# Weight conversion: first Prelu pass dense in float32, second pass in place, hi parts rounded by VectorE

## The chip, the cores and the metric

The kernel runs on one core of one Trainium2 chip. The metric is the device time of one execution in microseconds (us). It is measured several times for each kernel, and the median is given. The engines are PE (TensorE: matmuls, with the weight load PEld beside it), ACT (ScalarE), DVE (VectorE), POOL (GpSimd) and SP, which issues the transfers. Each engine works through its own list of instructions in order, and waits at an instruction until what it needs is there.

## What is computed

Attention with pooled keys and values for 8 batches of 8 heads with 576 tokens each, then a gated MLP over all 4608 tokens:

```python
k_p = k.reshape(B, H, Sp, pool, D).mean(axis=3)          # 72 pooled keys of 576
v_p = v.reshape(B, H, Sp, pool, D).mean(axis=3)
scores = scale * np.matmul(q, k_p.transpose(0, 1, 3, 2))
attn = np.exp(scores - np.max(scores, axis=-1, keepdims=True))
attn = attn / (np.sum(attn, axis=-1, keepdims=True) + 1e-09)
x = np.matmul(attn, v_p)                                  # tokens as rows: 4608 x 512
xn = x / np.sqrt(np.mean(x * x, axis=-1, keepdims=True) + 1e-06) * rms_g
g = xn @ w_gate                                           # 512 x 1536
out = (g * (1.0 / (1.0 + np.exp(-g))) * (xn @ w_val)) @ w_out
```

The three weight matrices arrive as float64, and the kernel has to turn them into float32 itself.

## The kernel before

**Stages.** The 4608 tokens make nine blocks of 512 (block 0 to 8); the 1536 columns of the MLP make twelve slices f of 128. Attention is done batch by batch, in four pairs of heads. A long string of steps, ORDER, written out by hand, sets the order of the work on every engine: each step issues its instructions on the engines that it uses, and an engine meets them in the order of the string. While block 0 goes through the MLP slice by slice, the weights of each slice are loaded and converted just ahead of it, and the attention of batches 0 and 1 (later 2) runs between the slices. Block 0 is through with that at about 200 us. From block 3 on, matrix products of seven factors in place of eight are used (lines 905 and 985); no weight is converted there.

**float32 in two parts.** Each float32 operand of the MLP is split into hi (rounded to the type fp32r) and lo (the rest, in fp32r too), and each product is three matmuls: hi by hi, lo by hi, hi by lo.

**The conversion.** The float64 weights are cut into 26 chunks (CHUNKS): for W1 (gate and value columns of a slice, 1024 columns a partition) and W2 (512 columns), with slices 0 and 11 of W1 in two halves of 512. So there are 16 chunks of 512 columns and 10 of 1024. The steps of a chunk n, in ORDER as a letter and the chunk's digit:

- `_l` w_load (L321, on SP): loads the raw eight-byte words, shifted by three bytes, so that the top byte of each float64 (sign and upper exponent bits) lies where an int8 can be read, eight bytes from one element to the next.
- `_a` w_bend (L327, on ACT): a Prelu over these int8, which folds the sign away from the exponent. It writes its result as bfloat16 back into the raw tile `wx`, again eight bytes from one element to the next.
- `_b` w_top (L336, on ACT): a second Prelu that reads these bfloat16 and writes int32, dense, into a tile `wt`: sign and exponent bits of the float32. The tile lies in `out0` or `out1` for chunks of 512 columns, and in a free W2 place for chunks of 1024.
- `_c` w_join (L340, on DVE): puts the mantissa bits of the raw word under them; `wt` is now float32, and the raw tile is free for the next load.
- `_h` w_hi (L354, on ACT): copies `wt` to fp32r, the hi part, in the weights' place `w`.
- `_w` or `_W` w_lo (L305, on DVE, or on POOL in pieces of 256 columns): `wt` less hi, the lo part.

**Around it.** ACT also does the exponentials of batches 0 and 1 (L451: five pieces of 72 columns for each head, straight out of PSUM), copies of transposed probabilities (L552, L554), squares of x (L600), the Silu (L1047) and hi parts of activations (L1085). Matmuls wait on these: scores and attention outputs share the eight PSUM banks with the MLP, and a bank is free only when ACT or DVE has read it.

Of the kernel before, what the change touches and what calls it, by code (L numbers as in the profile page):

```python
# [1219 lines left out]
```

## Time and profile before

| | before |
|---|---|
| device time, median of 3 runs | 1000.03 us (998.05 to 1000.80) |
| profiled execution | 998.13 us |
| its span, first to last instruction | 996.4 us |
| PE busy | 956.7 us (96% of the span) |
| DVE busy | 666.6 us (67%) |
| ACT busy | 540.6 us (54%) |
| POOL busy | 482.6 us (48%) |

These shares are means over the whole span, which has two very different parts: until about 200 us the weights are converted, and after that PE hardly ever stops. The rows below split the span there. "PEclk" is the share of full speed (2.4 GHz) that TensorE's clock was granted; it has two levels, 1.2 and 2.4 GHz, so 0.85 for a stretch says that it ran at the lower one for part of it.

### The profile page before, as it was taken

Reading aid. Unit: us, or ns where it says so; the run is one execution under the profiler, and the core shown is the slowest. Engines: PE = TensorE matmul, PEld = TensorE weight load, DVE = VectorE, ACT = ScalarE, POOL = GpSimd, SP = SyncE. Lnnn points to the kernel's source line nnn. Section 1 sums busy time; section 2 is a strip of 40 time slices with the busy share of each in tenths; the row PEclk is TensorE's granted clock in tenths of the full one; section 3 lists DMA queues with packets and bytes.
Section 4 is the critical chain, followed back from the end, with each engine's and each line's share of the span. In section 5 each row is a group of like instructions: output and inputs, shape, how many; then the busy total and the mean of one; then the engine's idle time right before and its main releaser. Section 6 shows DMA issues by size and latency. Waiting matters only on the chain.

```text
span 996.4 us, 14144 instructions
## 1 busy us (share of the span) xinstructions
PE 956.7 (96%) x4670; PEld 758.5 (76%) x4670; DVE 666.6 (67%) x1084; ACT 540.6 (54%) x955; POOL 482.6 (48%) x618
## 2 busy tenths in 40 slices
PE   7777988999999999999999999999999999999998
PEld 7466766877777787777777777878778778888886
DVE  6435756788889689878877868746566785442433
ACT  6899989854564655755446455541534552212332
POOL 3324543711231323442335688741276896245786
PEclk7579999999999999999999999999999999999999
DMA  9425666566667756977978776657786575766646
GB/s 290 154 99 174 232 228 183 189 203 202 199 212 216 221 146 195 302 238 230 291 223 270 217 234 219 215 188 250 237 275 188 159 235 171 219 212 206 215 142 208
DMA packets 142296, 211.40 MB, mean 212 GB/s; under 512 B 12240, under 2 KB 78288, under 8 KB 142224
## 3 DMA queue, kind: packets, MB, share of 16 engines
q1 hardware_dynamic: 142224, 210.51, 68.0%
q8 instruction: 37, 0.61, 0.3%
q14 instruction: 35, 0.29, 0.1%
HBM read 154.23 MB, written 56.23 MB: 211 GB/s over the span
## 4 chain that ended last, share of the span: by engine, by line
PE 69%; POOL 5%; DVE 3%; ACT 3%; DMA 3%; issue 1%; SPq 0%; DVEq 0%; ACTq 0%
PE pxy L905 30%; PE pf L985 14%; PE psg L1069 13%; PE po L1103 6%; PE psx L570 3%; PE pss L488 3%; POOL fp L305 2%; POOL xp L305 1%; DMA wp<-blocks 1%; ACT wx L327 1%; DMA pt<-rows 1%; DMA out<-o 1%; POOL w L305 1%; DVE xraw L654 0%; ACT wt L336 0%
## 5 line engine op out<-in xcount | busy, mean ns | idle before, releaser
L905 PE MATMUL pxy<-xp,wp 128*128 128x512 f32 x1512 | 361.2, 391 | 1.7 <-ACT o L1114 0.8
L905 PEld LDWEIGHTS pxy<-xp,wp 128*128 128x128 f32 x1512 | 282.4, 188 | 65.5 <-issue 2.9
L985 PE MATMUL pf<-fp,ring 128*128 128x512 f32 x756 | 189.6, 393 | 1.8 <-DVE fu L305 0.8
L1069 PE MATMUL psg<-xh,w 128*128 128x512 f32 x544 | 172.4, 399 | 6.8 <-ACT prob L451 6.1
L985 PEld LDWEIGHTS pf<-fp,ring 128*128 128x128 f32 x756 | 139.7, 188 | 38.0 <-issue 2.7
L1069 PEld LDWEIGHTS psg<-xh,w 128*128 128x128 f32 x544 | 101.9, 191 | 32.6 <-ACT prob L451 7.4
L1069 PE MATMUL psg<-xl,w 128*128 128x512 f32 x272 | 107.1, 394 | 0.0
L305 POOL TENSOR_TENSOR hl<-act,hh 128x256 fp32r<-128x256 f32 x58 | 46.9, 830 | 115.8 <-ACT hh L1085 94.6
L305 POOL TENSOR_TENSOR fp<-fs,fp 128x256 fp32r<-128x256 f32 x108 | 81.1, 777 | 41.0 <-ACT fp L958 37.2
L305 POOL TENSOR_TENSOR fp<-act,fp 128x256 fp32r<-128x256 f32 x72 | 55.0, 785 | 82.3 <-ACT fp L958 81.0
L305 POOL TENSOR_TENSOR w<-wt,w 128x256 fp32r<-128x256 f32 x50 | 43.2, 892 | 73.8 <-ACT w L354 73.8
L1103 PE MATMUL po<-w,hh 128*128 128x512 f32 x288 | 74.0, 394 | 0.0
L1103 PEld LDWEIGHTS po<-w,hh 128*128 128x128 f32 x288 | 55.1, 191 | 11.9
L305 POOL TENSOR_TENSOR fp<-hb,fp 128x256 fp32r<-128x256 f32 x68 | 54.5, 827 | 13.6 <-ACT fp L958 13.6
L1069 PEld LDWEIGHTS psg<-xl,w 128*128 128x128 f32 x272 | 51.7, 190 | 11.3
L1164 ACT COPY hb<-pxy 128x512 f32<-128x512 f32 x36 | 21.0, 587 | 72.1 <-PE pxy L905 72.1
L340 DVE SCALAR_TENSOR_TENSOR wt<-wx,wt 128x512 uint32<-128x512 uint32 (+1 forms) x26 | 23.5, 908 | 48.0 <-ACT wt L336 46.1
L958 ACT CAST fp<-act 128x512 fp32r<-128x512 f32 x36 | 22.2, 619 | 58.3 <-DVE act L1172 49.0
L958 ACT CAST fp<-fs 128x512 fp32r<-128x512 f32 x54 | 33.1, 618 | 34.6 <-POOL fs L305 17.5
L327 ACT ACTIVATE wx<-wx,shift 128x512 bf16<-128x512 int8 (+1 forms) x26 | 48.9, 1893 | 4.7 <-DMA wx<-w 4.7
L1171 DVE TENSOR_TENSOR u<-u,pxy 128x512 f32<-128x512 f32 x36 | 24.7, 685 | 39.7 <-PE pxy L905 39.5
L305 POOL TENSOR_TENSOR fs<-act,hb 128x256 f32<-128x256 f32 x32 | 23.3, 751 | 50.4 <-DVE act L1172 28.0
(194 smaller groups left out, 1634.0 us busy)
## 6 DMA issues: line engine op xcount, KB each, us to landing
wp<-sum SPq DMA_DIRECT2D x144, 256.0 KB
wp<-blocks SPq DMA_DIRECT2D x108, 256.0 KB
ring<-vs SPq DMA_DIRECT2D x72, 256.0 KB
ring<-vB SPq DMA_DIRECT2D x54, 256.0 KB
sum<-wt SPq DMA_DIRECT2D x48, 256.0 KB
blocks<-w SPq DMA_DIRECT2D x24, 512.0 KB
wx<-w SPq DMA_DIRECT2D x10, 1023.6 KB
v<-vN SPq DMA_DIRECT2D x32, 288.0 KB
```

The costliest lines, as they stand in the source:

```text
L305: getattr(eng, op)(*(x[..., o:o + step] for x in (out, a, b)))
L327: nc.scalar.activation(u, z, AF.Prelu, bias=shift[:, 0:1], alpha=SMALL)
L340: nc.vector.scalar_tensor_tensor(u, raw["x", n][0], 5, u, ALU.logical_shift_right, ALU.bitwise_or)
L488: nc.tensor.matmul(s["ps", h][:, t * SP:(t + 1) * SP], s["q"][r, o:o + P], s["pk"][r, :], start=True, stop=True)
L570: nc.tensor.matmul(ps[r, :n], s["pv"][:, r], x, start=True, stop=True)
L905: nc.tensor.matmul(ps[:, :NB], w[:, a, c, :], x[:, b, c, :], start=j == 0 and not more, stop=j == len(todo) - 1, skip_group_check=more)
L958: nc.scalar.copy(y[:, 0], f_source(i, k, j))
L985: nc.tensor.matmul(ps[c], w[:, a, c * P:(c + 1) * P], x[:, b], start=j == 0 and n == 0 and not more, stop=j == HALF - 1 and n == 2, skip_g ...
L1069: nc.tensor.matmul(ps[:, :NB], w[:, c, cols], x[c], start=(j == 0), stop=(j == len(todo) - 1))
L1103: nc.tensor.matmul(po[i][t], x[i, f][:, t * P:(t + 1) * P], w, start=(f == 0 and k == 0), stop=(f == NF - 1 and k == 2))
L1164: cp=lambda i, f: S_.copy(later(i, f), st["XY", i, f, 0]),
L1171: v1=lambda i, f: V.tensor_add(u2(i, f), u2(i, f), st["XY", i, f, 5]),
```

## The change

Three things change in the conversion, and nothing else:

1. `w_bend` writes float32, dense, into the tile `wt`, where it wrote bfloat16 into the raw tile. `wt` is therefore taken at this step, one step earlier than before (in ORDER the digit of the tile, such as `/0`, moves from `_b` to `_a`).
2. `w_top` reads that tile and writes it in place.
3. The hi parts are copied by VectorE (`nc.vector.tensor_copy`) in place of ScalarE.

```diff
-        raw["x", n] = x[:, :, 0], x.bitcast(I8)[:, :, 4], x.bitcast(BF16)[:, :, 2]
+        raw["x", n] = x[:, :, 0], x.bitcast(I8)[:, :, 4]
 
     def w_bend(n):
-        _, z, u = raw["x", n]
-        nc.scalar.activation(u, z, AF.Prelu, bias=shift[:, 0:1], alpha=SMALL)
-
-    def w_top(n):
         f, j = CHUNKS[n]
         if j == 3:
             t = space2(f + 1 if f < 3 else NF - 1 - f % 2, [P, 2 * WC], F32, f"wt{n}")
         else:
             t = two([P, WC], F32, tag="out", name=f"wt{n}")
         raw["t", n] = t
-        nc.scalar.activation(t.bitcast(I32), raw["x", n][2], AF.Prelu, scale=UNIT, bias=shift[:, 1:2], alpha=1.0 / SMALL)
+        nc.scalar.activation(t, raw["x", n][1], AF.Prelu, bias=shift[:, 0:1], alpha=SMALL)
+
+    def w_top(n):
+        t = raw["t", n]
+        nc.scalar.activation(t.bitcast(I32), t, AF.Prelu, scale=UNIT, bias=shift[:, 1:2], alpha=1.0 / SMALL)
 ...
-        nc.scalar.copy(parts[:, 0, :], raw["t", n])
+        nc.vector.tensor_copy(parts[:, 0, :], raw["t", n])
```

The steps of ORDER stand in the same order as before; the string is only wrapped anew, which moves the line numbers by five (L336 becomes L331, L340 becomes L335, L354 becomes L349; L327 stays). What moves is which engine's list an instruction stands in. A number behind a name is a tile's own number; a wait in brackets names the engine or the transfer queue whose progress is waited for.

**ScalarE, at about 48 to 56 us.** Here two chunks of 512 columns and one of 1024 go through both passes, between squares of x (L600) on which PE waits. Before:

```order
L327 ACTIVATE wx_467<-wx_467,shift 128x512 [waits DMAHW7_49]
L336 ACTIVATE wt_470<-wx_467,shift 128x512 [waits Activation_49]
L327 ACTIVATE wx_424<-wx_424,shift 128x1024 [waits DMAHW5_49]
L600 ACTIVATE own_170<-psx_1_0_445 128x288 [waits PE_49]
L327 ACTIVATE wx_475<-wx_475,shift 128x512 [waits DMAHW0_49]
L336 ACTIVATE wt_483<-wx_424,shift 128x1024 [waits Activation_49]
L600 ACTIVATE own_139<-psx_2_0_417 128x288
L336 ACTIVATE wt_486<-wx_475,shift 128x512 [waits Activation_49,Pool_49]
```

After:

```order
L327 ACTIVATE wt_469<-wx_467,shift 128x512 [waits DMAHW7_49]
L331 ACTIVATE wt_469<-wt_469,shift 128x512 [waits Activation_49]
L327 ACTIVATE wt_473<-wx_424,shift 128x1024 [waits DMAHW5_49]
L595 ACTIVATE own_170<-psx_1_0_445 128x288 [waits PE_49]
L327 ACTIVATE wt_480<-wx_476,shift 128x512 [waits DMAHW0_49,Pool_49]
L331 ACTIVATE wt_473<-wt_473,shift 128x1024 [waits Activation_49]
L595 ACTIVATE own_139<-psx_2_0_417 128x288
L331 ACTIVATE wt_480<-wt_480,shift 128x512 [waits Activation_49]
```

The instructions stand in the same order. The wait for POOL, which frees the tile `out0`, has moved from the second pass to the first.

**ScalarE, at about 74 to 84 us.** The Silu of slice 0, then hi parts and passes, then the exponentials of batch 1. Before:

```order
L1047 ACTIVATE act_0_611<-act_0_611 128x512 [waits DVE_49]
L354 CAST w_3_614<-wt_550 128x1024
L336 ACTIVATE wt_632<-wx_530,shift 128x512 [waits Activation_49,Pool_49]
L354 CAST w_3_637<-wt_632 128x512 [waits DVE_49,Pool_49]
L449 ACTIVATE early<-early 128x5 [waits DVE_49]
L451 ACT_TABLE_LOAD [waits PE_49]
L451 ACTIVATE prob,early<-pss_1_0_620,early 128x72 [waits Activation_49]
```

After:

```order
L1042 ACTIVATE act_0_613<-act_0_613 128x512 [waits DVE_49]
L331 ACTIVATE wt_584<-wt_584,shift 128x512 [waits Activation_49]
L444 ACTIVATE early<-early 128x5 [waits DVE_49]
L446 ACT_TABLE_LOAD [waits PE_49]
L446 ACTIVATE prob,early<-pss_1_0_622,early 128x72 [waits Activation_49]
```

Both copies have left ScalarE's list.

**VectorE, at about 39 to 46 us**, ahead of the first matmuls of the MLP, which need `w_0` and the lo part `xl` of x. Before:

```order
L340 SCALAR_TENSOR_TENSOR wt_386<-wx_303,wt_386 128x512
L340 SCALAR_TENSOR_TENSOR wt_388<-wx_288,wt_388 128x1024
L1033 SCALAR_TENSOR_TENSOR xl_0_393<-psx_0_1_378,gmean,xh_0_383 128x224
L429 TENSOR_REDUCE own_170<-v_1_415 72x128
L554 COPY own_178<-pst_3_2_411 72x2x64
L305 TENSOR_TENSOR w_0_422<-wt_386,w_0_422 128x512
L473 RECIPROCAL early<-early 128x5
L1033 SCALAR_TENSOR_TENSOR xl_2_443<-psx_2_0_417,gmean,xh_2_441 128x288
```

After:

```order
L335 SCALAR_TENSOR_TENSOR wt_349<-wx_305,wt_349 128x512
L335 SCALAR_TENSOR_TENSOR wt_321<-wx_290,wt_321 128x1024
L349 CAST w_0_317<-wt_273 128x512
L1028 SCALAR_TENSOR_TENSOR xl_0_393<-psx_0_1_380,gmean,xh_0_385 128x224
L349 CAST w_1_404<-wt_321 128x1024
L349 CAST w_0_422<-wt_349 128x512
L424 TENSOR_REDUCE own_170<-v_1_415 72x128
L549 COPY own_178<-pst_3_2_411 72x2x64
L300 TENSOR_TENSOR w_0_422<-wt_349,w_0_422 128x512
L468 RECIPROCAL early<-early 128x5
L1028 SCALAR_TENSOR_TENSOR xl_2_443<-psx_2_0_417,gmean,xh_2_441 128x288
```

Three copies now stand between the joins and the lo part of x.

## Rows read from the trace of the kernel before

**Rows 1.** Busy time by stretch: span, PE, PEld, DVE, ACT, POOL, PEclk, DMA.

```profile
0.00:200.00 200.00, 169.86 (x870) 132.43 (x870) 116.63 (x194) 171.87 (x345) 84.73 (x108) 0.85 0.60 194
200.00:350.00 150.00, 149.55 (x776) 117.55 (x775) 123.04 (x232) 82.57 (x152) 36.81 (x45) 1.00 0.68 207
350.00:996.00 646.00, 637.33 (x3029) 508.56 (x3027) 426.98 (x660) 286.20 (x460) 361.06 (x465) 1.00 0.71 219
```

**Rows 2.** Timeline of PE: start, duration, instruction, idle time before and its releaser.

```profile
55.91 1.23 PE L570 MATMUL psx<-own 72*64 72x288 f32 x4 [5.97 <-ACT own L600]
...
88.30 1.60 PE L1103 MATMUL po<-w,hl 128*128 128x512 f32 x4 [4.60 <-ACT prob L451]
...
92.71 0.62 PE L1069 MATMUL psg<-xh,w 128*128 128x512 f32 x2
...
95.46 1.10 PE L1103 MATMUL po<-w,hl 128*128 128x512 f32 x4
...
98.27 0.63 PE L546 MATMUL pst<-ident,prob 128*72 128x128 f32 x4
...
129.91 1.22 PE L1069 MATMUL psg<-xh,w 128*128 128x512 f32 x2 [2.38 <-ACT prob L451]
...
159.87 0.73 PE L1069 MATMUL psg<-xh,w 128*128 128x512 f32 x2 [3.74 <-ACT prob L451]
```

**Rows 3.** Groups by line and shape: busy, mean ns of one, idle before.

```profile
L327 ACT ACTIVATE wx<-wx,shift 128x1024 bf16<-128x1024 int8 x10 | 26.1, 2607 | 0.0
L327 ACT ACTIVATE wx<-wx,shift 128x512 bf16<-128x512 int8 x16 | 22.9, 1446 | 4.7 <-DMA wx<-w 4.7
...
L1169 ACT ACTIVATE hb<-hb 128x512 f32<-128x512 f32 x36 | 22.7, 632 | 42.1 <-DVE hb L1168 42.0
...
L336 ACT ACTIVATE wt<-wx,shift 128x512 int32<-128x512 bf16 x16 | 12.1, 757 | 0.5
L336 ACT ACTIVATE wt<-wx,shift 128x1024 int32<-128x1024 bf16 x10 | 12.1, 1209 | 0.3
...
L354 ACT CAST w<-wt 128x1024 fp32r<-128x1024 f32 x10 | 10.5, 1046 | 0.5 <-DVE wt L340 0.5
L354 ACT CAST w<-wt 128x512 fp32r<-128x512 f32 x16 | 9.9, 621 | 2.5 <-DVE wt L340 2.5
```

**Rows 4.** The same view, groups of DVE.

```profile
L647 DVE RECIPROCAL acc<-acc 128x288 f32<-128x288 f32 x12 | 23.2, 1943 | 2.4 <-ACT acc L644 2.4
...
L340 DVE SCALAR_TENSOR_TENSOR wt<-wx,wt 128x1024 uint32<-128x1024 uint32 x10 | 12.5, 1254 | 12.1 <-ACT wt L336 12.1
...
L812 DVE TENSOR_TENSOR vsum<-vsum 128x256 f32<-128x256 f32 x24 | 11.5, 481 | 0.4
...
L340 DVE SCALAR_TENSOR_TENSOR wt<-wx,wt 128x512 uint32<-128x512 uint32 x16 | 11.1, 691 | 35.8 <-ACT wt L336 34.0 <-issue 1.6
...
L1114 DVE COPY o<-po 128x512 f32<-128x512 f32 x4 | 2.7, 682 | 1.4 <-DMA sum<-wt 1.4
```

**Rows 5.** L327 alone by stretch: span, busy ACT with count, PEclk, DMA.

```profile
47.60:55.90 8.30, 5.40 (x3) 0.91 0.40 136
...
129.90:159.90 30.00, 8.10 (x4) 0.95 0.66 210
```

**Rows 6.** L354 alone by stretch, the same columns.

```profile
55.90:88.30 32.40, 5.06 (x6) 0.81 0.26 93
88.30:129.90 41.60, 4.95 (x6) 0.96 0.71 241
129.90:159.90 30.00, 2.08 (x2) 0.95 0.66 210
```

**Rows 7.** Timeline of ACT, one row.

```profile
47.65 0.41 ACT L600 ACTIVATE own<-psx 128x288 f32<-128x288 f32 x1 [2.62 <-DVE xl L1033]
```

**Rows 8.** Timeline of POOL.

```profile
29.81 1.42 POOL L305 TENSOR_TENSOR w<-wt,w 128x256 fp32r<-128x256 f32 x2 [6.35 <-ACT w L354]
...
161.56 3.04 POOL L305 TENSOR_TENSOR w<-wt,w 128x256 fp32r<-128x256 f32 x2
```

More of the change, by code (lines that the diff above doesn't have):

```diff
@@ new lines @@
+xc400 lq42 sc42:03 me26:2 gt26 rc31 whb2/0 mx420/1 sb420 wsb1 ex420 whb3/1 dm41 rs31 vl26 Wlb3 mx421/1 sb421 mo25 av401:1
+ft301 sm420/0 xd40 hi26/0 Lo26 ex421 sm421/0 Wlb2 lq43 sc43:32 mx431/0 xc401 dp41/1 av411 xd41 mx430/1 xc411 av410:1
+xc410 lv42/1 wsb3 pv42/0 Wfb3 whb4/1 mg27:0 gt27 Nm421 Nm420 Wlb4 tr42/0 sb431 ex431 lk50 pk50/1 sb430 lv43/1 pv43/1
+sm431/1 ex430 sm430/1 me27:1 zt40/1 Nm430 zt41 vl27 Nm431 me28:0 mo26 dm42 sq40 lq50 tr43/0 wsb2 hi27/1 wsb4 Zf40 Zf41
+Lo27 zh41/1 Zl41 ft311 dp42/1 Zf42 Zf43 mg28:3 sc50:12 mx501/1 dm43 zh43/0 gt28 vl28 zl43 zs43 sb501 yh31 zs41 yl31
@@ new lines @@
+ys35 yh35 zh54/1 pr310 rl315/3 Zl54 cp31 mo2b pr312 lk52 pk52/0 rl304/1 yh34 Yl34 rl302/4 ev22/0 pr302 rl321/2 lv50/1
+sb511 sa31 ex511 st22 zs54 yl32 Yl35 pr320:0 pr304:4 ev21/0 pr315:7 rl301/7 sb510 sa30 rl311/4 sm511/0 pv50/0 ev20/1
+rl313/6 ex510 rl314/0 sm510/0 Nm510 pr301:6 u230 st21 st20 ev23/0 ys36 pr303 u330 pr313:1 c230 pr311:5 rl305/1 pr305:6
+yh36 zh51/1 pr314 Yl36 rl325/5 u231 Zl51 rl333/6 pr325 u331 c231 v231 lq52 v230 pr321:4 rl316/4 Nm511 sw30 vb30 pr316
+dp50/1 sw31 vb31 rm41:1 rl306/3 v131 rt41 rl324/7 va31 pr306 v130 sc52:25 va30 Fs310 fh300/5 Fl300 rl323/4 tr51/0 cp32
@@ new lines @@
+pm321 pr386 sw38 rl396/3 vb38 Fs332 rl394/7 pr394:0 fh332/4 rs50 Fs341 v138 xc611 sa38 Nm621 ft330 rl393/4 pr393:6 u339
+c239 sw39 rl3a3/1 Fl332 tr62/0 pr395:1 v239 lq63 rl392/6 pr392 av610:7 xc610 lv63/1 sq60 Fs342 pv63/0 ft331 sc63:20
+mx631/1 va38 rl3a1/2 fh322/7 dm62 rl3a4/7 mx630/1 pm330:76 sb631 ft332 _J10 sb630 rl3a5/0 sa39 pr396 v139 va39 pm331
+ex631 Fl322 dp62/0 Fs362 sm631/0 fh323/5 rl3b2/3 fh340/8 ft322 Nm631 pr3a0:0 cp3a vb39 pr3a3:2 rl3b0/5 Fs333 ex630
+sm630/0 Fs343 pr3a1:1 fh333/6 pr3a4:3 Fl333 pm322 Fs363 sq61/0 pm332 Nm630 tr63/1 Fl323 dm63 u23a u33a c23a sw3a Fl340
@@ new lines @@
+fh360/3 oe30 rl523/6 Fl354 ys56 sw50 Qd30 yh56 Yl56 qf30/0 fh362/5 rl514/3 Fl360 lv70/1 u351 pr514:4 Nm701 c251 ft354
+sw51 qf31/1 v250 pv70/1 lq71 pm354 rl515/0 pr515 v251 ft355 rl520/2 pm355 qg31 ex700 ft360 rl524/3 sm700/1 qg30 pr520:4
+Nm700 pr506 v150 cp52 rl530/7 va50 rl516/0 pr523:5 Fl362 Fl363 pr516 pm360 v151 fh500/4 tr70/0 ft361 rl525/1 rl526/6
+pr521:2 u252 vb50 u352 rl522/5 pr524:7 c252 ft362 pr522 fh361/8 Fl361 pr525 v252 sc71:75 va51 mx711/0 rl531/2 mx710/1
+pm361 rm61:2 Fl500 sb711 ex711 pm362 Fs510 fh364/7 dm70 fh510/8 sb710 pr526 v152 ex710 rl533/4 ft363 pm363 rl534/5
@@ new lines @@
+pm710:76 rl766/2 pr766 rl762/5 pr762 ft704 rl790/4 v176 og51 sw76 rl780/3 rl781/1 Fs715 pm704 vb76 Fs730 Fs740 fh713/7
+ft712 Fl713 rl772/0 pm711 ft713 pr780:1 pr790:0 ft705 cp78 Fl712 pm712 sa76 va76 fh714/6 pr781:2 fh720/3 u278 pm713 Fl720
+rl773/6 pr772 ft714 pr773:2 pm705 rl782/3 pr782 ft715 rl784/7 fh715/8 Fl714 qa70 pm714 u377 sa77 rl774/2 pr774 ft720
+fh740/4 rl775/0 qa71 c277 pr775 v277 Fl715 pm715 qb70 Fl740 rl783/1 rl776/4 pr776 v177 sw77 vb77 rl793/2 pm720 cp79
+rl785/5 pr784 ft721 fh730/8 Fl730 va77 rl794/0 pr783:7 u378 rl792/4 Fs731 ft730 c278 qb71 sw78 Fs760 fh721/7 Fs741
@@ L237 @@
+qg70 fh761/8 fh762/5 ft761 Fl761 ft762 fh763/4 Fl763 Fl762 fh764/6 pm761 ft764 ft763 ft765 qg71 Fl764 og70 og71 oe71
+pm762 pm763 fh765/7 Fl765 pm764 of70 pm765 qh70 qh71 oh70 oh71
 """
```

312 lines of the change are left out of this document (140 added, 172 removed).

## The prediction

> **What bounds the kernel now.** I first read the busy time by stretch [rows 1]. From 200 us on PE works 149.55 of 150 us, and 637.33 of the last 646: there is nothing to win there, and the change touches no instruction there, since all 26 chunks are converted by then. Until 200 us PE works 169.86 of 200 us, at a clock of 0.85 of full speed, while ACT is the busiest engine with 171.87 us. So the whole matter is how much sooner PE gets through the first stretch; whatever it gains there, the rest moves up by. Next I read where PE waits, in its timeline [rows 2]. Four long waits stand after the first 45 us, 5.97, 4.60, 2.38 and 3.74 us, 16.7 us together, and each ends with an ACT instruction: a square of x (L600) once, an exponential of batch 1 (L451) three times. These are not the results of the conversion. They stand behind conversion work in ACT's list. Each wait also costs clock: the twelve matmuls from 88.30 to 92.71 take 4.41 us, the same twelve from 95.46 to 98.27 take 2.81 [rows 2], so 1.6 us is lost at the lower level after a wait.
>
> **Part 1, the first pass.** It costs 1.446 us for 512 columns and 2.607 for 1024 [rows 3], 2.27 ns for each further column, while the second pass pays 0.88 ns (1.209 less 0.757 over 512). The second pass reads two-byte elements eight bytes apart and writes four-byte words side by side; the first reads one-byte elements eight bytes apart and writes two-byte ones eight bytes apart. So the spread-out read is not what is dear, unless one byte is another matter than two; the spread-out write is. Written densely I price the first pass as the second today: 16 × 0.757 + 10 × 1.209 = 24.2 us against 49.0, a saving of 24.8. The bounds are 0 (the read of bytes is what is dear) and 28.4 (16 × 0.632 + 10 × 1.046 = 20.6, the rate with both sides dense [rows 3]).
>
> The Trainium skill (SBUF — State Buffer, "Door 1: The DMA port swizzle") speaks against this part: it says that accesses run at full rate if two of them hit each 16-byte line, so that bfloat16 may be spread by eight elements at no cost. Here the spread is four. By that rule the write is free already, the first pass stays as it is, and the sum is rival A's. The read in the second pass runs at full rate at that spread [rows 3], as the rule has it; for the 2.27 ns of the first pass the rule has no reason.
>
> **Part 2, the second pass.** In place and dense: 0.632 and 1.046 instead of 0.757 and 1.209 [rows 3], 24.2 less 20.6 = 3.6 us; at worst nothing.
>
> **Part 3, the hi copies.** ACT loses 16 × 0.621 + 10 × 1.046 = 20.4 us [rows 3]. DVE gets 26 copies that the trace does not show. Nearest are its copy of 512 columns out of PSUM, 0.682, and the join's 1.254 for 1024: 16 × 0.682 + 10 × 1.254 = 23.4 us, which I take. If it moved two columns at a time they would cost as much as operations of half the width (0.481 and 0.691 [rows 4]), 14.6 us. Its slowest one-input row, the reciprocal with 1.943 us for 288 columns, 6.7 ns each, is the other bound: 16 × 3.45 + 10 × 6.9 = 124 us. A copy follows its join on the same engine, so it waits for no other engine's result; what is queued behind it is only later by its length. DVE has 116.6 us to do in the first 200 [rows 1], with the copies 140.
>
> So ACT is freed of 24.8 + 3.6 + 20.4 = 48.8 us, or of 20.4 at the least. What of it reaches PE I sum up wait by wait.
>
> **Until 56 us.** Between 47.6 and 55.9 ACT does three first passes, 5.40 us [rows 5], two of 512 and one of 1024, and no hi copy: 2 × 0.69 + 1.40 = 2.8 off, and 0.3 from the two second passes, 3.1. Ahead of that, from 12 to 45 us, ACT is freed of five copies (4 × 0.62 + 1.05 = 3.5 us), four first passes (3 × 0.69 + 1.40 = 3.5) and some 0.5 on second passes, 7.5 us. But DVE gets the copies in its two unbroken runs, three of them (0.68 + 1.25 + 0.68 = 2.6 us) right between the joins and the lo part of x, for which ACT already waits 2.62 us at 47.65 [rows 7], and PE, ACT and POOL hand heads to each other there. That is worth between −2.6 (only these copies count) and 3.5 (7.5 less the 4.0 of five copies on DVE); I take 2, as ACT's list shows next to no gaps there. Together 5, of a wait of 5.97 and what lies ahead of it.
>
> **From 56 to 88 us.** ACT sheds 5.06 us of copies [rows 6]; four of the six (3.8 us) and three first passes (2.8) stand between 66.9 us, where it waited for PE, and the exponentials that PE waits for. 6.6 us against a wait of 4.60: it goes, and with it the 1.6 of clock, 6.2. Next late is PE itself.
>
> **To 130 and to 160 us.** 4.95 us of copies alone [rows 6] cover the wait of 2.38, with 1.6 of clock (taken from the first one) 4.0. In the last stretch 2.08 of copies [rows 6] and half of 8.10 of first passes [rows 5], four of them, 4.2, are 6.3 against 3.74: with the clock 5.3.
>
> **Taken back.** (a) The first pass now waits for the tile `wt`. At nearly all places its last reader is done long before, but for a W2 chunk at about 163 us it is a lo part on POOL that ends about then; POOL's pair of subtractions takes 1.42 us undisturbed and 3.04 then [rows 8], so ACT may wait up to 1.6 us there, and with it the Silu and exponentials behind. (b) From 160 to 200 us DVE is busy 31 of 40 us, and seven copies (5.3 us) make that 36 while PE stops nowhere: a wait or two of about a microsecond. I take 2.5 for both. 5.0 + 6.2 + 4.0 + 5.3 − 2.5 = 18.0 us. That is off the profiled execution, 998.13 us, which gives 980.1; it lies 1.9 below the median of the runs, so from that 1000.0 − 18.0 = **982 us**.
>
> **Rivals.** *A, the dense write doesn't make the first pass cheaper.* For: no other instruction here reads single bytes. Against: the second pass's cheap read at the same step. Then only 20.4 us of copies and at most 3.6 leave ACT. The first wait keeps most of its length (I put 1.5 for 5), but the copies alone cover the next two, and with the lead from them also the fourth: 1.5 + 6.2 + 4.0 + 5.3 − 2.5 = 14.5, **985.5 us**.
>
> *B, copies and POOL's subtractions hold each other up.* For: POOL's pairs already stretch from 1.42 to 3.04 us [rows 8]. Against: PE has room until 160 us. If each copy costs 0.6 to 0.75 more, 1.25 and 2.0, DVE needs 31 + 6 × 1.25 + 2.0 = 40.5 of the 40 us from 160 to 200, and 26.4 + 9.8 = 36.2 of the 36 to 38 that PE needs from 88 to 130; DVE ends late in both and I take half of the gain away, 9 us: **991 us**. The Trainium skill (SBUF — State Buffer, "Who interferes with whom") says that copies and casts of VectorE can take the port pair shared with GpSimd for a whole instruction, and that the other engine then stands still. No row here shows such a copy.
>
> *C, slower: VectorE becomes the bound of the first stretch.* Place: its list until 200 us. It decides once 116.6 us and 26 copies fill the 200 us, at 3.2 us a copy. At the reciprocal's rate it would need 241 us, 41 more: **1041 us**. Against it: writing fp32r costs DVE nothing extra in its two-input rows, and ACT's casts run at its full rate.
>
> *D, no change:* the waits move to DVE in all four places, and the gain is used up within 3 us: **999 us**.
>
> **Chances.** Forecast 0.55 (own range 977 to 988), A 0.22, B 0.12, D 0.06, C 0.05. A measurement of this kernel can tell about 0.3%, 3 us. Faster by more than that: forecast, A and B, less some tail of B, 0.87; the same 0.07; slower 0.06. The range reaches down to 973, if the start gains 3.5 instead of 2, nothing is taken back, and a denser start brings 5 us of the clock that is missing in the first stretch, 0.15 of 200 us [rows 1] (18 + 1.5 + 2.5 + 5 = 27), and up to 992, which takes in A and B and leaves out C, D and a tail.
>
> **What would show it.** L327 at about 0.76 and 1.21 us (A: unchanged); L331 at 0.63 and 1.05; the copy on DVE at 0.7 and 1.25 or below (B: over 1.2; C: over 3.2). In PE's timeline the waits at 88, 130 and 160 us are gone and the one at 56 us is about half; the last weight conversion, now at 193 us, ends near 175; from there on PE works without a stop as before. ACT's busy time falls from 541 to about 492 us and DVE's rises from 667 to 680 to 690. I am wrong if PE finds new waits on DVE or POOL before 200 us that sum to more than a few microseconds, or if it no longer runs through between 200 and 350 us, where DVE is busy 123 of 150 us [rows 1] and has to keep up with a PE that comes 18 us sooner.

## The result

The changed kernel takes 986.0 us (median, 985.5 to 986.8) beside 1000.4 of the kernel before, measured with it: a ratio of 0.9859, 95% interval 0.9839 to 0.9880, 14.4 us less. The profiled execution takes 986.45 us with a span of 984.7, so 11.7 less than the profiled one of before.

Busy time by stretch, as in [rows 1]:

```profile
0.00:200.00 200.00, 178.26 (x948) 138.10 (x949) 147.65 (x252) 140.37 (x338) 92.32 (x110) 0.90 0.65 208
200.00:350.00 150.00, 150.00 (x777) 118.66 (x776) 122.39 (x228) 83.41 (x148) 40.41 (x51) 1.00 0.67 203
```

PE does 178.26 us of work in the first 200 in place of 169.86, ACT 140.37 in place of 171.87, DVE 147.65 in place of 116.63; from 200 to 350 us PE still runs through. The prices of the conversion, as in [rows 3] (busy, mean ns of one | idle before):

```profile
L327 ACT ACTIVATE wt<-wx,shift 128x1024 f32<-128x1024 int8 x10 | 12.3, 1233 | 2.8 <-DMA wx<-w 2.8
...
L327 ACT ACTIVATE wt<-wx,shift 128x512 f32<-128x512 int8 x16 | 12.0, 756 | 7.2 <-DMA wx<-w 5.4 <-DVE w L300 1.9
...
L331 ACT ACTIVATE wt<-wt,shift 128x1024 int32<-128x1024 f32 x10 | 11.5, 1154 | 0.2
...
L331 ACT ACTIVATE wt<-wt,shift 128x512 int32<-128x512 f32 x16 | 11.5, 720 | 0.3
...
L349 DVE CAST w<-wt 128x512 fp32r<-128x512 f32 x16 | 8.3, 518 | 0.1
L349 DVE CAST w<-wt 128x1024 fp32r<-128x1024 f32 x10 | 8.3, 829 | 0.0
```

The first pass has halved (24.3 us in place of 49.0), the second has hardly moved (23.0 us in place of 24.2), and the copies cost DVE 16.6 us. The waits of PE, as in [rows 2]:

```profile
51.94 0.71 PE L565 MATMUL psx<-own 72*64 72x288 f32 x4 [4.05 <-ACT own L595]
...
78.50 0.47 PE L1098 MATMUL po<-w,hl 128*128 128x512 f32 x1 [0.37 <-ACT prob L446]
80.22 0.96 PE L1098 MATMUL po<-w,hl 128*128 128x512 f32 x3 [1.25 <-DVE act L1038]
...
86.61 1.43 PE L1098 MATMUL po<-w,hl 128*128 128x512 f32 x4 [0.89 <-POOL hl L300]
...
144.84 1.22 PE L1064 MATMUL psg<-xh,w 128*128 128x512 f32 x2 [2.40 <-ACT prob L446]
```

The first wait is down from 5.97 to 4.05 us, and the last from 3.74 to 2.40. Of the two in between, the one at 130 us is gone; the one at 88 us (now 78.50) is 0.37, with 1.25 and 0.89 us behind it that wait for DVE and POOL. Two more are new, 1.29 us for DVE at 42 us (shown below) and 0.30 for POOL at 122.

**How far PE is ahead.** The rest is told by one measure: how much earlier than in the profiled execution of before PE starts the same group of instructions, at six places. One of them, in before and then in after:

```profile
164.31 0.60 PE L546 MATMUL pst<-ident,prob 128*72 128x128 f32 x4
```

```profile
149.25 0.60 PE L541 MATMUL pst<-ident,prob 128*72 128x128 f32 x4
```

PE is 15.06 us ahead there. The table gives this for all kernels; the column "span" is 996.4 less the span, the places are times of before. The medians come from five measurements, in which before took 1000.1 to 1001.6 us; a ratio is always to the before of the same measurement. "First five" and "other 21" say which engine makes these hi copies; the first pass is as in before or dense.

| kernel | first pass | first five | other 21 | 57 | 88 | 143 | 164 | 201 | 745 | span | median us |
|---|---|---|---|---|---|---|---|---|---|---|---|
| after | dense | DVE | DVE | 4.5 | 9.8 | 13.9 | 15.1 | 15.3 | 13.5 | 11.7 | 986.0 |
| copy_only | before | DVE | DVE | −2.3 | 0.7 | 2.8 | 0.0 | 0.3 | 0.5 | −0.3 | 998.9 |
| dense_only | dense | ACT | ACT | 7.0 | 9.9 | 16.0 | 17.6 | 18.6 | 14.7 | 13.5 | 984.7 |
| copy_early | dense | DVE | ACT | 3.9 | 6.8 | 12.9 | 14.3 | 15.3 | 14.9 | 13.7 | 984.5 |
| copy_late | dense | ACT | DVE | 5.9 | 10.7 | 14.7 | 19.6 | 15.4 | 15.8 | 14.1 | 983.8 |
| load_early | dense | DVE | DVE | 2.3 | 7.6 | 11.7 | 16.5 | 12.4 | 13.2 | 12.5 | 984.3 |
| square_first | dense | DVE | DVE | 6.5 | 8.9 | 13.0 | 16.0 | 11.9 | 10.9 | 9.8 | 987.3 |
| late_pair | dense | DVE | DVE | 4.1 | 8.3 | 12.1 | 17.0 | 15.5 | 13.3 | 12.6 | 983.3 |
| late_pair_act | dense | ACT | ACT | 6.5 | 9.3 | 14.4 | 19.1 | 17.0 | 16.0 | 14.6 | 983.4 |
| late_pair_21 | dense | ACT | DVE | 5.2 | 10.2 | 14.3 | 19.1 | 17.7 | 16.9 | 16.6 | 983.6 |
| late_chain | dense | ACT | DVE | 6.5 | 12.0 | 16.0 | 20.9 | 19.3 | 20.4 | 19.1 | 983.4 |

Every row is one execution. load_early has the program of after up to some 115 us, yet is 2.2 us behind it at 57: a single entry is good to some two microseconds. The step from one column to the next within a row is the surer reading: from 57 to 88 us it is 5.3 in both, and 4.2 in late_pair, the same program to there too, so it is good to about one. Two more kernels, spread_f32 and half_word, differ from after only in where the first pass writes and the second reads.

### The profile page after: what moved, and what is told of

It reads as the page before. It is cut to its first block, busy times and chain, and to the rows that moved or that the text cites. A ratio compares the mean times of both kernels' runs of the same rounds, so it can differ in the third digit from the quotient of the medians.

```text
span 984.7 us, 14142 instructions
## 1 busy us (share of the span) xinstructions
PE 950.6 (97%) x4670; PEld 752.8 (76%) x4670; DVE 680.9 (69%) x1110; ACT 499.1 (51%) x929; POOL 490.1 (50%) x618
## 4 chain that ended last, share of the span: by engine, by line
PE 76%; DVE 5%; DMA 5%; ACT 3%; POOL 3%; issue 2%; SPq 1%; DVEq 0%; ACTq 0%; POOLq 0%
PE pxy L900 31%; PE psg L1064 15%; PE pf L980 14%; PE po L1098 8%; PE psx L565 3%; PE pss L483 3%; DMA ring<-vs 1%; DMA wp<-blocks 1%; POOL xp L300 1%; DMA wx<-w 1%; PE psr L657 1%; DMA pt<-rows 1%; POOL w L300 1%; ACT wt L327 1%; DMA wp<-sum 1%
## 5 line engine op out<-in xcount | busy, mean ns | idle before, releaser
L300 POOL TENSOR_TENSOR w<-wt,w 128x256 fp32r<-128x256 f32 x50 | 47.1, 971 | 49.5 <-DVE w L349 49.5
L300 POOL TENSOR_TENSOR fp<-hb,fp 128x256 fp32r<-128x256 f32 x68 | 54.4, 827 | 13.7 <-ACT fp L953 13.7
L1166 DVE TENSOR_TENSOR u<-u,pxy 128x512 f32<-128x512 f32 x36 | 24.7, 685 | 42.3 <-PE pxy L900 42.1
L300 POOL TENSOR_TENSOR fs<-act,hb 128x256 f32<-128x256 f32 x32 | 23.4, 751 | 49.2 <-DVE act L1167 26.7
L1160 DVE TENSOR_TENSOR u<-hb,pxy 128x512 f32<-128x512 f32 x36 | 24.6, 684 | 33.3 <-PE pxy L900 19.6
L1098 PE MATMUL po<-w,hl 128*128 128x512 f32 x144 | 42.1, 402 | 2.5 <-DVE act L1038 1.2
```

The source lines that it names most:

```text
L300: getattr(eng, op)(*(x[..., o:o + step] for x in (out, a, b)))
L1098: nc.tensor.matmul(po[i][t], x[i, f][:, t * P:(t + 1) * P], w, start=(f == 0 and k == 0), stop=(f == NF - 1 and k == 2))
L1160: u2=lambda i, f: V.tensor_add(u2(i, f), later(i, f), st["XY", i, f, 1]),
L1166: v1=lambda i, f: V.tensor_add(u2(i, f), u2(i, f), st["XY", i, f, 5]),
```

## Experiments: which part of the change did it

The theory after the result was that the dense pass and the copies carry about half each. Two kernels do one part each. copy_only is the kernel before with

```diff
-        nc.scalar.copy(parts[:, 0, :], raw["t", n])
+        nc.vector.tensor_copy(parts[:, 0, :], raw["t", n])
```

> The kernel before with the hi copies on VectorE and nothing else: both Prelu passes as before. Theory (the dense first pass carries about half of the gain): ScalarE loses 20.4 us of copies and keeps 49 us of first passes; PE, which in the changed kernel is 15 us earlier at 200 us, is 6 to 10 us earlier here, and the time is 989 to 994 us. Rival 1 (the copies alone cover the waits of PE, as the hand sum for the rival with an unchanged first pass had it): 985 to 987 us, the time of the changed kernel. Rival 2 (the copies lengthen VectorE's run ahead of the first matmuls of the MLP and hand the gain back there): the wait at 56 us grows beyond 6 us and the time is 996 us or more.

Measured: 998.9 us, ratio 0.9978 (0.9962 to 0.9995), about 2 us. That is rival 2's time, though the wait that it names did not grow beyond 6 us (5.70, below). dense_only is the changed kernel with that line put back:

> The changed kernel with the hi copies back on ScalarE: only the two Prelu passes are changed. Theory (both parts are needed, the gains are about additive): ScalarE is freed of some 25 us, first passes at 0.76 and 1.23 us, PE 6 to 10 us earlier at 200 us, 988 to 993 us; the wait near 52 us is shorter than the changed kernel's 4.05, since VectorE has no copies ahead of the lo part of x. Rival (the copies on VectorE bring nothing, what they free on ScalarE they cost on VectorE): 986 us or less. Other rival (without the copies moved, ScalarE remains what PE waits for and the dense pass is hidden): 996 us or more.

Measured: 984.7 us, ratio 0.9843 (0.9819 to 0.9867). The theory fell: the passes alone bring all of it, and the rival "the copies on VectorE bring nothing" holds. PE's waits in copy_only show why 20 us less on ACT are worth so little:

```profile
58.19 1.23 PE L570 MATMUL psx<-own 72*64 72x288 f32 x4 [5.70 <-ACT own L600]
...
87.65 0.47 PE L1103 MATMUL po<-w,hl 128*128 128x512 f32 x1 [1.63 <-ACT prob L451]
...
129.53 0.73 PE L1069 MATMUL psg<-xh,w 128*128 128x512 f32 x2 [1.44 <-ACT prob L451]
...
159.14 1.22 PE L1069 MATMUL psg<-xh,w 128*128 128x512 f32 x2 [3.87 <-ACT prob L451]
```

The waits at 88 and 130 us are shorter than in [rows 2], 1.63 and 1.44 us in place of 4.60 and 2.38; but PE comes 2.3 us late to the first one, which is still 5.70 us, and the last one, 3.87, has not shrunk at all (ahead of it ACT waited 2.91 us for a load, as it does in after, see below). In dense_only:

```profile
49.42 0.76 PE L565 MATMUL psx<-own 72*64 72x288 f32 x4 [2.26 <-ACT own L595]
...
78.45 1.15 PE L1098 MATMUL po<-w,hl 128*128 128x512 f32 x4 [2.87 <-ACT prob L446]
...
142.38 1.22 PE L1064 MATMUL psg<-xh,w 128*128 128x512 f32 x2 [2.20 <-ACT prob L446]
```

**Where the copies cost.** In after PE has a wait for DVE ahead of the MLP's first matmuls that neither before nor dense_only has:

```profile
42.13 1.23 PE L565 MATMUL psx<-own 72*64 72x288 f32 x4 [1.29 <-DVE own L424]
```

ACT's square behind the last lo part of x, in after and then in dense_only:

```profile
46.22 0.41 ACT L595 ACTIVATE own<-psx 128x288 f32<-128x288 f32 x1 [4.77 <-DVE xl L1028]
```

```profile
43.66 0.41 ACT L595 ACTIVATE own<-psx 128x288 f32<-128x288 f32 x1 [2.62 <-DVE xl L1028]
```

With the copies on DVE, ACT waits 4.77 us, without them 2.62, as in [rows 7]. DVE's list in after has the copies right ahead of what PE and ACT wait for (the sum into `own`, at 40.78 us, stands behind the first three):

```profile
38.23 0.42 DVE L349 CAST w<-wt 128x512 fp32r<-128x512 f32 x1
...
38.92 1.94 DVE L349 CAST w<-wt 128x1024 fp32r<-128x1024 f32 x2
...
43.97 1.20 DVE L424 TENSOR_REDUCE pv<-v 72x128 f32<-72x1024 f32 x1
45.09 0.74 DVE L415 TENSOR_REDUCE pk<-k 128x72 f32<-128x576 f32 x1
45.75 0.43 DVE L1028 SCALAR_TENSOR_TENSOR xl<-psx,gmean,xh 128x224 fp32r<-128x224 f32 x1
```

The next two kernels split the copies at this place: copy_late leaves the first five on ACT, copy_early, the other way round, puts only these on DVE.

```diff
-        nc.vector.tensor_copy(parts[:, 0, :], raw["t", n])
+        (nc.scalar.copy if n in (0, 1, 2, 3, 5) else nc.vector.tensor_copy)(parts[:, 0, :], raw["t", n])
```

> The changed kernel with the first five hi copies (the ones that stand before PE's first matmuls of the MLP) on ScalarE as before, the other 21 on VectorE. Theory (the copies cost on VectorE in its unbroken run before 46 us and are worth something later): PE is 7 to 8 us earlier than before at 57 to 79 us, as with the dense pass alone, the waits of 2.87 us at 78 and of 2.20 us at 142 that the dense pass alone shows get shorter, PE 19 to 22 us earlier at 200 us, and 980 to 983.5 us. Rival (copies on VectorE bring nothing later either, since VectorE's own results take ScalarE's place in what PE waits for): 984 to 986 us, the time of the dense pass alone.

> The other half: the changed kernel with the first five hi copies on VectorE and the other 21 on ScalarE. Theory: VectorE's run until 46 us is longer by them, ScalarE waits over 4 us for the last lo part of x as in the changed kernel, PE loses 2 to 3.5 us by 57 us against the dense pass alone, and the relief later is missing too: 986 to 989 us. Rival (where the copies stand does not matter): 984 to 986 us, as the dense pass alone and the changed kernel.

Measured: 983.8 us, ratio 0.9824 (0.9807 to 0.9841), and 984.5 us, ratio 0.9843 (0.9817 to 0.9870). copy_late lies 0.3 us above the theory's range, and its lead at 200 us is 15.4 us, not 19 to 22: the two waits named did get shorter (1.27 us, now for DVE, and 0.35), but a later one took the gain back ("the wait that stayed", below). copy_early has the rival's time, with the theory's loss at 57 us (3.9 against 7.0). The two are too near to each other to be told apart by their times.

The traces do tell the start: with the first five copies on DVE (after, copy_early, load_early, late_pair, spread_f32 with 4.0 and half_word with 3.4; square_first, whose order differs here, left out) PE is 2.3 to 4.5 us ahead at 57 us, in the five dense kernels with them on ACT 5.2 to 7.0. The means are 3.7 and 6.2: the five copies cost 2.5 us there. The steps within the rows show where. From the group at 43.20 us of before to the one at 45.32, every kernel with these copies on DVE loses 1.55 to 1.57 us of its lead, at the wait for DVE shown above, and no other loses any; from there to 57 us, at the wait for squares, the six kernels with them on DVE gain 1.6 to 2.5 us and the five others 2.5 to 3.1.

The other 21 are worth next to nothing as long as the pass is dense: from 57 to 143 us PE gains 9.4 in after, 8.8 in copy_late, 9.0 in dense_only, 9.0 in copy_early, and 7.9 to 9.5 in the other dense kernels that keep this order, with the copies on either engine. With the old pass (copy_only) it is 5.1. So pass and copies relieve the same two waits, and the pass alone does all of it.

## Experiments: why the first pass was dear

The passes carry the result, so what made the old one cost 2.27 ns a column matters. It wrote two-byte elements eight bytes apart; the new one writes four-byte elements side by side. Two kernels change one of these each. spread_f32 is copy_only with

```diff
-        raw["x", n] = x[:, :, 0], x.bitcast(I8)[:, :, 4], x.bitcast(BF16)[:, :, 2]
+        raw["x", n] = x[:, :, 0], x.bitcast(I8)[:, :, 4], x.bitcast(F32)[:, :, 1]
```

> The kernel before with the hi copies on VectorE, and with the first pass writing float32 into the upper word of each raw pair (four bytes, a step of eight bytes) in place of bfloat16 (two bytes, the same step); the second pass reads those words from there. It tells whether it is the step or the two-byte element that made the first pass cost 2.27 ns a column. Theory (the step, each element written apart): L327 stays at 1.45 and 2.61 us or goes up, and the time is that of the kernel with only the copies moved. Rival (the two-byte write into a four-byte word): L327 falls to about 0.76 and 1.23 us and the time is within 3 us of the changed kernel's 986.

half_word is the changed kernel with

```diff
-        nc.scalar.activation(t, raw["x", n][1], AF.Prelu, bias=shift[:, 0:1], alpha=SMALL)
+        u = raw["u", n] = t.bitcast(mybir.dt.bfloat16).rearrange("p (n o) -> p n o", o=2)[:, :, 0]
+        nc.scalar.activation(u, raw["x", n][1], AF.Prelu, bias=shift[:, 0:1], alpha=SMALL)
...
-        nc.scalar.activation(t.bitcast(I32), t, AF.Prelu, scale=UNIT, bias=shift[:, 1:2], alpha=1.0 / SMALL)
+        nc.scalar.activation(t.bitcast(I32), raw["u", n], AF.Prelu, scale=UNIT, bias=shift[:, 1:2], alpha=1.0 / SMALL)
```

> The changed kernel with the first pass writing bfloat16 into the lower half of each word of the dense tile (two bytes, a step of four bytes), read from there by the second pass. The other half of the same question. If the two-byte write into a word is what is dear: L327 at 1.45 and 2.61 us, 2.27 ns a column, and 989 to 994 us. If the step of eight bytes is what is dear: L327 at 0.76 and 1.23 us, and 986 us as the changed kernel.

The groups of the first pass in spread_f32 and half_word (copy_only has the prices of [rows 3], 2607 and 1443 ns):

```profile
L327 ACT ACTIVATE wx<-wx,shift 128x1024 f32<-128x1024 int8 x10 | 12.4, 1236 | 2.4 <-DMA wx<-w 2.4
...
L327 ACT ACTIVATE wx<-wx,shift 128x512 f32<-128x512 int8 x16 | 12.1, 766 | 4.7 <-DMA wx<-w 4.7
```

```profile
L328 ACT ACTIVATE wt<-wx,shift 128x1024 bf16<-128x1024 int8 x10 | 14.7, 1465 | 2.4 <-DMA wx<-w 2.4
...
L328 ACT ACTIVATE wt<-wx,shift 128x512 bf16<-128x512 int8 x16 | 13.8, 872 | 7.1 <-DMA wx<-w 5.3 <-DVE w L300 1.8
```

From 512 to 1024 columns, a further column costs 2.27 ns with two bytes at a step of eight, 0.92 with four bytes at a step of eight, 1.16 with two bytes at a step of four, and 0.93 in after. So neither the step nor the two-byte element alone is dear; both together are. The expectations had each of the two as the whole cause, and both were wrong for half_word: the step of four costs a little more than dense, and no more. That 1.16 is half of 2.27 would fit one price for every eight bytes of the tile that get only part of a word; this is a guess that no run tests. The times follow: 985.5 us, ratio 0.9834 (0.9810 to 0.9859), and 984.5 us, ratio 0.9836 (0.9812 to 0.9860). A float32 write into the raw tile would have done as well as the dense one. And since the second pass of spread_f32 is not in place (0.762 and 1.231 us), working in place is not what brings the time.

The Trainium skill (SBUF — State Buffer, "Door 1: The DMA port swizzle") says that accesses run at full rate when at least two hit each 16-byte line, and lets bfloat16 be spread by eight elements for free. Four bytes at a step of eight agree with it (0.92 ns); two bytes at the same step, as many accesses in each line, do not (2.27 ns), and the measurement decides.

## Experiments: the wait that stayed

PE's wait at 145 us (160 in before) was to go. ACT's list ahead of these exponentials has a wait that was not there before, for the raw weights of chunk k:

```profile
133.39 1.24 ACT L327 ACTIVATE wt<-wx,shift 128x1024 f32<-128x1024 int8 x1 [2.80 <-DMA wx<-w]
...
151.59 0.77 ACT L327 ACTIVATE wt<-wx,shift 128x512 f32<-128x512 int8 x1 [1.88 <-DVE w L300]
```

SP issued this load at 124.76 us, behind stores of weight sums that wait for DVE (not for ScalarE, as the expectation below has it), and ACT's pass starts 8.6 us after that:

```profile
115.24 4.33 SPq L784 DMA_DIRECT2D sum<-wt  x2
...
123.88 0.82 SPq L784 DMA_DIRECT2D sum<-wt  x2
124.76 0.68 SPq L316 DMA_DIRECT2D wx<-w  x1
```

load_early issues it ahead of two of these stores (_lk is the load, _cg the join that frees its tile, ws23 and ws21 are the stores):

```diff
-_u5 _cg _E121
+_u5 _cg _lk _E121
...
-_hg ws23 ws21 _Wg _g6 _u6 _V12/0 _D122 _lk _k20
+_hg ws23 ws21 _Wg _g6 _u6 _V12/0 _D122 _k20
```

> The changed kernel with one load of raw weights (chunk k, W1[10]) issued on SP right behind the join that frees its tile, ahead of two stores of weight sums that wait for ScalarE. Theory (the fourth wait stayed because ScalarE waited 2.80 us for this load with exponentials queued behind): that wait of ScalarE and PE's wait of 2.40 us at 145 us fall to under 0.5 us, PE gains 2 to 3.5 us there, and the time is 982.5 to 984.5 us. Rival (something else is late next in the same place, such as VectorE's maxima or the wait for the tile of chunk l): 985.5 to 987 us.

Measured: 984.3 us, ratio 0.9830 (0.9808 to 0.9853). PE in load_early:

```profile
144.84 0.73 PE L1068 MATMUL psg<-xh,w 128*128 128x512 f32 x2 [0.35 <-ACT prob L450]
...
153.89 2.12 PE L487 MATMUL pss<-pk,q 64*128 64x72 f32 x18 [1.93 <-ACT pt L551]
```

The wait for exponentials has gone from 2.40 to 0.35 us, and PE gains 4.9 us between 143 and 164 us of before, where after gains 1.2. But 9 us later stands a new wait of 1.93 us, and the 18 matmuls behind it take 2.12 us, with a granted clock of 0.71 from 150 to 160 us; in after the same 18 have next to no wait and take 1.33, and the clock there is 1.00:

```profile
153.64 1.33 PE L483 MATMUL pss<-pk,q 64*128 64x72 f32 x18 [0.24 <-ACT pt L547]
```

By 201 us 4.1 of the 4.9 us are gone. The second wait was hidden behind the first: the time is in the theory's range, but the gain is not what the theory said it would be.

The late issue is not the whole cause of the first wait. copy_late has the load where after has it, issued at 123.92 us, and shows the same picture as load_early (ACT, then PE):

```profile
129.67 1.23 ACT L327 ACTIVATE wt<-wx,shift 128x1024 f32<-128x1024 int8 x1
```

```profile
141.81 0.73 PE L1064 MATMUL psg<-xh,w 128*128 128x512 f32 x2 [0.35 <-ACT prob L446]
...
150.88 1.49 PE L483 MATMUL pss<-pk,q 64*128 64x72 f32 x18 [1.98 <-ACT pt L547]
```

ACT doesn't wait, 5.75 us after the issue; PE gains 4.9 us from 143 to 164, too, and has lost 4.1 of them by 201. In the six others that have a cheap first pass and the load in its old place (after, dense_only, copy_early, square_first, spread_f32, half_word) ACT starts 8.2 to 8.6 us after the issue, having waited 1.5 to 2.8. So the first wait hangs on how long this load takes, and the early issue takes that off the path; why it landed sooner in this one execution is not known.

In load_early ACT stood ahead of the second wait, for the tile `wt`:

```profile
151.85 0.77 ACT L331 ACTIVATE wt<-wx,shift 128x512 f32<-128x512 int8 x1 [2.14 <-DVE w L304]
...
153.28 1.04 ACT L551 COPY pt<-pst 72x512 f32<-72x512 f32 x2
```

late_pair moves both passes of chunk m (_am, _bm), which wait for that tile, behind the copies of transposed probabilities (_D131, _D130) for which PE waits:

```diff
-_lm/1 _am/1 _bm _T131:1/1 _o7 _D131 _hk _T130 _D130 _q20
+_lm/1 _T131:1/1 _o7 _D131 _hk _T130 _D130 _am/1 _bm _q20
```

Three kernels have both moves, and differ in where the copies are:

> The changed kernel with the early load of chunk k, and with both Prelu passes of chunk m, which wait about 2 us for a tile that VectorE's lo part of chunk l frees, moved behind the two copies of transposed probabilities that stood behind them in ScalarE's list. Theory (two waits of PE in series, 6 us apart; with the load alone the first went and the second, 1.93 us and its clock, came up in its place): both are gone, the 4 to 5 us that PE wins at 145 to 150 us last until 200 us, and the time is 980 to 983 us. Rival 1 (a third result is as late, POOL's lo parts or ScalarE's squares): PE is not over 16 us ahead at 200 us, 984 to 986 us. Rival 2 (what PE has won at 200 us beyond some 14 us is given back by late transfers): ahead by 17 us or more at 200 us, but 984 to 986 us.

> The same two moves with the first five hi copies on ScalarE and 21 on VectorE. Theory: it has the start of the dense pass alone (PE 6 to 7 us ahead at 57 us) and neither of the two late waits, 19 to 21 us ahead at 200 us, 978 to 981 us. Rivals as for the run before: 983 to 985 us.

> The same two moves with all 26 hi copies on ScalarE, so that of the change only the dense and in-place passes are left. Theory (with the start undisturbed and the two late waits moved out of the way, ScalarE's 20 us of copies show again): waits of PE for exponentials at 78 and 142 us of 2 to 3 us each remain, the time is 1 to 4 us above the run with 21 copies on VectorE. Rival (the copies are worth nothing on VectorE anywhere): the same time as that run within 1 us.

Measured: 983.3, 983.6 and 983.4 us, ratios 0.9827 (0.9801 to 0.9853), 0.9830 (0.9803 to 0.9858) and 0.9822 (0.9797 to 0.9847). Where the copies stand makes no difference that these runs can tell, which is the rival's outcome for late_pair_act; late_pair_21 misses its 978 to 981 us and its lead (17.7 at 201 us) and has the rivals' time. The wait of 1.93 us is gone (0.57 to 1.09 us for the next copy is left), and in the two kernels with copies on DVE a third has come up, this time for DVE. In late_pair:

```profile
144.37 0.73 PE L1068 MATMUL psg<-xh,w 128*128 128x512 f32 x2 [0.35 <-ACT prob L450]
...
159.36 0.73 PE L1068 MATMUL psg<-xh,w 128*128 128x512 f32 x2 [1.75 <-DVE prob L504]
```

PE is 17.0 us ahead at 164 and 15.5 at 201, which is rival 1's case by the lead; the time lies between the theory's and the rival's. DVE's maxima and differences of batch 2 stand behind three sums of weight blocks:

```profile
154.69 1.75 DVE L766 TENSOR_TENSOR wsum<-w 128x1024 f32<-128x1024 f32 x1
156.47 1.72 DVE L775 TENSOR_TENSOR wsum<-wsum 128x256 f32<-128x256 f32 x2
158.12 0.52 DVE L500 TENSOR_REDUCE mx<-pss 128x5 f32<-128x360 f32 x1
158.77 0.53 DVE L504 TENSOR_TENSOR prob<-pss,mx 128x360 f32<-128x360 f32 x1
```

late_chain, from late_pair_21, moves them ahead:

```diff
-Wt3/1 Wf30 _A131 _Y131 Wf31 lv21/0 mx201/1 sb201
+mx201/1 sb201 Wt3/1 Wf30 _A131 _Y131 Wf31 lv21/0
```

> The kernel with the two late moves and 21 copies on VectorE, and besides VectorE's maxima and differences of one head of batch 2 moved ahead of three sums of weight blocks that stood before them in its list. Theory (a chain of late results, each of which comes to light when the one before is mended: exponentials at 145 us, transposed copies at 151, then a wait of 1.76 us at 157 us for VectorE's differences): the third wait goes too, PE keeps the 19 to 20 us that it is ahead at 164 us until 200 us, and the time is 980.5 to 982.5 us. Rival 1 (the sums of weight blocks, now later, hold up stores and products in their turn): PE falls back below 18 us ahead by 220 us. Rival 2 (what is gained beyond some 16 us goes into transfers after 500 us): 19 us or more at 200 us and a time of 983 to 984.5 us.

Measured: 983.4 us (979.1 to 985.3), ratio 0.9824 (0.9798 to 0.9850). In its profiled execution, the 979.1, this wait is gone too, but some 6 us behind its place stands a fourth, for POOL, that late_pair_21 does not have:

```profile
163.50 0.61 PE L661 MATMUL psr<-one,acc 128*128 128x1 f32 x4 [1.34 <-POOL acc L304]
```

PE falls from 20.9 us ahead at 164 to 19.3 at 201, and keeps that to the end. From 143 to 201 us it gains 3.3 us, where late_pair and late_pair_21 gain 3.4: the higher lead comes from the first 143 us, in which late_chain's program is late_pair_21's. The other five executions took 982.6 to 985.3, and have no trace; the median and the lead are rival 2's case. The 979.1 comes from a better start and from next to no loss behind 200 us, and this edit touches neither. So a chain of late results is shown, four by now, but that their removal makes the kernel faster is not: the medians of this and the other dense kernels are 983.3 to 984.7 (square_first apart) against 986.0 of after, but the intervals of the ratios overlap.

square_first goes for the wait at 52 us: VectorE's two pooling sums behind the last lo part of x, ACT's squares ahead of three conversions.

```diff
-_V10/0 _m000:7 _K11/1 _Y021 _x21 _y21 _Z21 _m010:6 _D031 _l7/0 _a7/1 _b7 _c7 _a4 _Z10 _ld/1 _l6 _ad/0 _m002 _b4 _Z20 _bd _A011:5
+_m000:7 _Y021 _x21 _y21 _V10/0 _K11/1 _Z21 _Z20 _m010:6 _D031 _l7/0 _Z10 _ld/1 _l6 _m002 _A011:5
...
-_Z30 _cd _c4 _x10 _A031:4 _Z31 _P01
+_Z30 _x10 _A031:4 _Z31 _a7/1 _b7 _c7 _a4 _ad/0 _b4 _bd _cd _c4 _P01
```

> The changed kernel with VectorE's two pooling sums moved behind the last lo part of x (the steps V10 and K11), and ScalarE's squares of x moved ahead of the conversions of chunks 7, 4 and d, which stand between them. Theory (PE's wait of 4.05 us at 52 us is for squares that stand behind conversions in ScalarE's list and behind VectorE's run): that wait falls to under 1 us and PE is 3 to 5 us earlier at 60 us than in the changed kernel; the conversions come later and some of it returns as waits at 80 to 100 us: 982 to 984.5 us. Rival (PE stands at the first matmuls that need the converted chunks instead, all of it returns): 985.5 to 988 us.

Measured: 987.3 us (983.1 to 988.4), ratio 0.9850 (0.9827 to 0.9873). The wait is gone and PE is 6.5 us ahead at 57 us, but only 4.5 at 79, where after has 5.6. PE stands in between for DVE's share of the norm:

```profile
59.30 1.04 PE L545 MATMUL pst<-ident,prob 128*72 128x128 f32 x4 [1.37 <-DVE total L666]
61.20 2.40 PE L685 MATMUL psb<-ident,r 128*128 128x128 f32 x10 [0.87 <-DVE r L676]
```

At 164 us it is 16.0 us ahead, and 4.1 of these are gone by 201, at a wait of 1.95 us for transposed copies, the one that load_early and copy_late have. The time is the rival's outcome, by other waits than the rival named.

## Point by point

- **Part 1** was right in mechanism and size: 0.756 and 1.233 us against 0.757 and 1.209, and 24.7 us saved against 24.8. That the spread-out write is dear holds for two-byte elements only. Rival A's condition did not come about.
- **Part 2** was mis-sized: 0.720 and 1.154 us in place of 0.632 and 1.046, so 1.2 us saved in place of 3.6. The price was taken from L1169 [rows 3], which works in place too, but with Silu and into float32, not with Prelu into int32.
- **Part 3**, the copies, cost DVE 16.6 us in place of 23.4. An undisturbed one takes 0.42 and 0.69 us, what DVE's operations of half the width take [rows 4], so the lower bound was the nearer one. Rival C was far off.
- **Until 56 us** the sum was 5.0, the measure 4.5. By place the split held: PE starts the MLP's first matmuls at 43.29 us in place of 45.32, 2.0 us sooner (2 forecast), and 2.5 come at the wait behind them (3.1 forecast). By part it hides two sides: the dense pass alone brings 7.0 in all (dense_only), and the first five copies take 2.5 of it back, the price that the lower bound had for them in DVE's run.
- **At 88 and 130 us** 6.2 and 4.0 were forecast, 11.2 and 15.2 in sum; PE is 9.8 and 13.9 ahead (8.5 at 98 us, behind the waits of 1.25 and 0.89 for DVE and POOL). The step that failed is the cause: I put these gains down to the copies, for the most part at 88 us and wholly at 130, and dense_only has them without (9.9 and 16.0). The sum left out the six first passes between 88 and 130 us, 13.39 us of ACT in before, and these cover the wait as well. So the sum came near at 130 us by luck: what it credited to the copies the dense pass did.
- The last conversion was to end near 175 us, ACT's busy time to fall to about 492, DVE's to rise to 680 to 690: the last hi copy ends at 177.9 (193.9 in before), and the busy times are 499.1 and 680.9. The new waits of PE for DVE and POOL before 200 us, 1.29, 1.25, 0.89 and 0.30, sum to 3.7 us, about the few microseconds that were allowed.
- **At 160 us** the sum had 5.3 less 2.5, 2.8; it was 1.4 (13.9 to 15.3). This is the term that failed by its mechanism: the wait stayed, for a load that SP issued late and that ACT got 8.6 us after its issue, which the sum did not look at (in copy_late it came sooner, and the wait went). What was taken back under (a) is there, 1.88 us of ACT, but at 152 us and for a lo part of DVE, not of POOL; and it would have cost PE its time only if the wait ahead had gone, as load_early and copy_late show.
- **After 200 us** the sum had no loss. The profiled execution loses 3.6 us from there to its end (15.3 to 11.7), scattered, the largest for transfers (1.8 us in three waits for `ring`, 1.2 in one for `pt`). Of what the other kernels are ahead at 201 us, between nothing (load_early) and 5.1 us (dense_only) is gone at the end, and no edit here aimed at it. What sets them stays open.
- **Rival A's time**, 985.5, is what came out, but its mechanism, copies alone with the first pass unchanged, was run as copy_only: 998.9 us. It failed at the first wait (1.5 forecast, −2.3 measured) and at the last (5.3, and it stayed). **B**: copies and POOL's subtractions do stretch each other; the six pieces at 38.73 us take POOL 5.67 us in after and 5.14 in dense_only, and the two copies beside them 1.94 us, where undisturbed ones take 0.42 and 0.69 (the 13 copies with no POOL instruction beside them take 0.42 to 0.43 and 0.65 to 0.69, nine of the other 13 longer, up to 0.95 and 1.22):

```profile
38.73 5.67 POOL L300 TENSOR_TENSOR w<-wt,w 128x256 fp32r<-128x256 f32 x6 [6.41 <-DVE w L349]
```

```profile
36.69 5.14 POOL L300 TENSOR_TENSOR w<-wt,w 128x256 fp32r<-128x256 f32 x6 [5.92 <-ACT w L349]
```

```profile
124.93 0.69 DVE L349 CAST w<-wt 128x1024 fp32r<-128x1024 f32 x1
```

  The 0.83 us more is about one of POOL's pieces (5.67 us for six), which fits the rule that the prediction quoted from the Trainium skill (SBUF — State Buffer, "Who interferes with whom": one engine stands still for the other's whole instruction); that it stood still is not shown. But on the mean the 26 copies take 0.10 to 0.14 us more than undisturbed ones, not the 0.6 to 0.75 that B needed.

The forecast was 982 us with a range of 973 to 992, and 986.0 came out; of the 3.6 us by which the gain fell short, 1.3 were missing by 143 us, 1.4 around 160, and the other 0.9 is what is left for the time behind 200 us, where the profiled execution lost more, 3.6.

## What to carry to other kernels

Work taken off the busiest engine counts only where its list ends last: price every wait by what is next late, among loads in SP's list too, because waits in series hide each other and mending one shows the next. When a change has two parts that relieve the same wait, run each part alone before crediting either; and before crediting an edit with a wait that went, look whether every kernel without the edit has it. Moving work to an engine with idle time costs where it lands ahead of a result that somebody waits for, so move only the instances that stand elsewhere.
